# Four open output tiles in block 0, later steps for batches 2 and 3, and a last output tile in two halves

## Chip, cores and metric

The kernel runs on one core of one Trainium2 chip. The metric is the device time of one execution in microseconds. It was run seven times; the profile is of one execution more closely looked at. "PE" is TensorE, "DVE" VectorE, "ACT" ScalarE, "POOL" GpSimd and "SP" the sync engine, whose instructions here are only DMA issues.

## The reference

Linear attention without softmax, a norm over each head, and a two-layer network with a leaky rectifier whose slope differs by column:

```
kv  = einsum('bhsd,bhse->bhde', k, v)          # 8 batches, 8 heads, 576 tokens, head size 64
out = einsum('bhsd,bhde->bhse', q, kv)
rms = sqrt(mean(out*out, axis=-1) + 1e-6)
x   = (out / rms * g_norm)                     # -> 4608 tokens x 512
h   = x @ w_in                                 # 512 x 2048
g   = max(h, 0) + alpha * min(h, 0)
y   = g @ w_out                                # 2048 x 512
```

Inputs and output are float32. The kernel loads with a cast to float16 and multiplies in float16.

## The kernel before

**Tiling.** The 4608 tokens of the output are nine blocks of 512 (`W`, index `w`); a batch has 576, so blocks and batches don't coincide. A block's first product gives 16 groups (`g`) of 128 hidden columns: `m1_group` runs four matmuls into a bank `h_ps`, and `m1_evac` empties it with one ScalarE instruction (`m_sb`) and one VectorE instruction (`gt`). The second product gives four output tiles of 128 tokens (`a`), each a sum of 16 matmuls (`y_mm`) in one bank; `y_out` copies it to SBUF and issues two DMAs on SP, as 64 rows are one run in the output. From block 2 on the loop runs group `g` of block `w` and then four `y_mm` of block `w - 1`. The eight banks of PSUM are three for `h_ps` (`ps_h`), one each in `ps_y` ("y") and `ps_s` ("s"), and three in `ps_o` ("o0" to "o2").

**Attention.** Batches come into two stages in turn by GpSimd DMAs (`load`, two DMAs for each of q, k, v). `regroup` copies q and k from a stage into another order, for batches 0 to 2 on VectorE and later on GpSimd (`regroup_batch`). `step_kv` builds k'v on TensorE, and VectorE masks it into `kv_sb`.

Batches 0 and 1 are transposed on TensorE (`step_t`), and x comes out transposed: `step_ot`, a square on ScalarE or VectorE, `ssq_mm` (a matmul with a mask sums the squares; Ln and Exp on ScalarE give `rstd`) and `norm` on VectorE. From batch 2 on q is transposed by a DMA on SP (`transpose_q`, gives `qtm`), and a tile of 128 tokens passes four steps: `tile_a` (four matmuls `otm_ps`, square on ScalarE into `sqm_sb`), `tile_b` (VectorE reduce into `ss`), `tile_c` (Ln, Exp on ScalarE, then `rg` on GpSimd), `tile_d` (VectorE product `xrow`, then a DMA transpose on SP into `xm`, which the block's first product reads).

**Order.** Nothing is scheduled by the framework: each engine runs its instructions in the order in which the program writes them. The steps of a later block's attention are spread over the loop of block `w` by `phase_steps(w + 1)`: a list of (begin, mid, end), one entry per group, whose parts run before the group, after the group's first product, and after its `y_mm`. Block 2 needs the last 128 tokens of batches 0 and 1 too (`step_tail_ot`, `step_tail_ssq`), so its list starts with these.

**Around the change.** Block 0 runs all its 16 groups first. Then `ahead` runs `y_mm` for three of its four output tiles, interleaved with the attention of batch 1, as filler while TensorE would wait. The fourth tile is done in block 1's loop, one `y_mm` per group. In block 1's loop also stand:

```
            if (w, g) == (1, 1):
                regroup(2, "q"); transpose_q(2)
            if (w, g) == (1, 3):
                nc.gpsimd.tensor_copy(out=gate[:], in_=qtms[2][0:1, 0, 0:1])
                load_batch(3); regroup(2, "k")
            if g == LOAD_G + 3 and w + 2 < B:      # g == 9
                regroup_batch(w + 2)
            if g == NF - 3 and w + 2 < B:          # g == 13
                transpose_q(w + 2)
```

The gate is a tiny GpSimd copy that waits for `qtm` of batch 2, so that the loads behind it on GpSimd start after it.

At the end, block 8's four output tiles run one after the other in the `ps_h` banks.

## Time and profile before

| | us |
|---|---|
| median of 7 runs | 304.66 |
| lowest, highest | 303.16, 305.23 |
| the profiled execution | 305.23 |
| its span in the trace | 303.2 |

| engine | busy, us | share of the span |
|---|---|---|
| PE | 284.8 | 94% |
| DVE | 169.7 | 56% |
| ACT | 152.9 | 50% |
| POOL | 97.8 | 32% |

The span is the traced part of the execution; 2.0 us lie around it. A view that lists instructions gives start and duration in us, the engine, the line, the output and inputs by their names in the program, and in brackets the idle time of the engine just before and what ended it. A wait is put down to the releaser that came last. Matmuls overlap, so one that lasts 0.38 us can be followed by the next after 0.22. The time to landing of a DMA counts from its issue.

### The profile page before, as it was taken

The numbers are of one execution on the slowest core, as the hardware profiler recorded it, in microseconds if no ns is written. First come the engines' busy times: TensorE is split into PE (matmuls) and PEld (weight loads), VectorE is DVE, ScalarE is ACT, GpSimd is POOL, SyncE is SP. The second block draws the span as 40 slices with busy tenths as digits, with TensorE's granted clock in tenths as the row PEclk, the third lists the DMA queues.
The fourth block names the chain that finished last, engine by engine and source line by source line (L and its number), as shares of the span: only waits on it lengthen the run. The fifth ranks groups of instructions, "written<-read, shape, count | busy, mean of one in ns | idle before, by whom it ended". The sixth has DMA issues, their size and how long they took to land.

```text
span 303.2 us, 4249 instructions
## 1 busy us (share of the span) xinstructions
PE 284.8 (94%) x1536; PEld 137.3 (45%) x1536; DVE 169.7 (56%) x261; ACT 152.9 (50%) x297; POOL 97.8 (32%) x109
## 2 busy tenths in 40 slices
PE   5899899883999999999999999999999999999993
PEld 2454444441554455445544544455445444444441
DVE  5469764773486448545963584459546744344200
ACT  1468357462385448435844574458437544434220
POOL 9823410095048414660565054614002300000000
PEclk9999999995799999999999999999999999999998
DMA  7999999699618971995389839935211411122133
GB/s 88 184 206 202 201 204 219 147 138 140 132 27 130 208 173 41 152 224 107 67 120 195 159 75 121 235 90 89 61 35 37 95 35 37 35 46 53 42 69 69
DMA packets 66068, 35.54 MB, mean 117 GB/s; under 512 B 32752, under 2 KB 61440, under 8 KB 66048
## 3 DMA queue, kind: packets, MB, share of 16 engines
q0 software_dynamic: 29664, 18.35, 43.9%
q1 hardware_dynamic: 36384, 16.93, 26.8%
q8 instruction: 12, 0.20, 0.3%
q14 instruction: 8, 0.07, 0.1%
HBM read 36.71 MB, written 9.44 MB: 152 GB/s over the span
## 4 chain that ended last, share of the span: by engine, by line
PE 74%; DMA 13%; issue 8%; POOL 3%; DVE 0%; ACT 0%; POOLq 0%; ACTq 0%
PE y_ps L487 37%; PE h_ps L465 33%; DMA w_in_sb<-in_moe_w_in_dram 5%; DMA w_out_sb<-in_moe_w_out_dram 5%; DMA kst<-in_k_dram 4%; PE otm_ps L387 2%; PE kv_ps L238 2%; POOL w_in_sb L161 1%; POOL qst L96 0%; POOL vst L100 0%; POOL kst L96 0%; POOL qst L100 0%; POOL rg L411 0%; DVE xrow L420 0%; DVE gt L474 0%
## 5 line engine op out<-in xcount | busy, mean ns | idle before, releaser
L474 DVE SCALAR_TENSOR_TENSOR gt<-m_sb,beta_sb,h_ps 128x512 f16<-128x512 f32 x144 | 105.8, 744 | 80.5 <-ACT m_sb L472 80.0
L487 PE MATMUL y_ps<-w_out_sb,gt 128*128 128x512 f16 x528 | 135.6, 380 | 0.0
L472 ACT ACTIVATE m_sb<-h_ps 128x512 f32<-128x512 f32 x144 | 85.5, 597 | 94.3 <-PE h_ps L465 93.7
L465 PE MATMUL h_ps<-xm,w_in_sb 128*128 128x512 f16 x448 | 115.1, 379 | 0.0
L465 PEld LDWEIGHTS <-w_in_sb 128*128 128x128 f16 x584 | 56.2, 99 | 69.1 <-issue 10.9
L487 PEld LDWEIGHTS <-gt 128*128 128x128 f16 x576 | 56.3, 98 | 67.0 <-issue 0.8
L411 POOL TENSOR_TENSOR rg<-ss,g_all 128x512 f32<-128x512 f32 (+1 forms) x30 | 31.2, 1045 | 83.0 <-ACT ss L409 83.0
L465 PE MATMUL h_ps<-xt,w_in_sb 128*128 128x512 f16 (+1 forms) x136 | 33.2, 386 | 6.4 <-DVE gt L474 6.4
L497 ACT COPY y_sb<-y_ps 128x512 f32<-128x512 f32 x33 | 19.2, 582 | 17.4 <-PE y_ps L487 17.1
L399 DVE TENSOR_REDUCE ss<-sqm_sb 128x8 f32<-128x512 f32 (+1 forms) x30 | 20.5, 682 | 9.4 <-ACT sqm_sb L393 9.3
L420 DVE TENSOR_TENSOR xrow<-otm_ps,rg 128x512 f16<-128x512 f32 (+1 forms) x30 | 20.4, 681 | 9.2 <-POOL rg L411 9.2
L393 ACT ACTIVATE sqm_sb<-otm_ps 128x512 f32<-128x512 f32 (+1 forms) x30 | 17.8, 592 | 8.6 <-PE otm_ps L387 8.5
L106 POOL COPY qsb<-qst 128x2560 f16<-128x2560 f16 x5 | 11.6, 2327 | 12.7 <-issue 10.0
L106 POOL COPY ksb<-kst 128x2560 f16<-128x2560 f16 x5 | 11.6, 2321 | 8.8 <-DMA kst<-in_k_dram 8.8
L387 PEld LDWEIGHTS <-qtm 128*128 128x128 f16 x120 | 9.2, 98 | 7.1
L238 PE MATMUL kv_ps<-vst,ksb 128*128 128x128 f16 x160 | 10.4, 219 | 1.7 <-DMA vst<-in_v_dram 1.2
L197 PE MATMUL warm_ps<-warm,mask 128*128 128x512 f16 x26 | 8.7, 474 | 3.3 <-DVE eps_t L140 3.3
L387 PE MATMUL otm_ps<-kv_sb,qtm 128*128 128x128 f16 x120 | 11.6, 219 | 0.0
L406 ACT ACTIVATE ss<-ss,eps_t 128x8 f32<-128x8 f32 (+1 forms) x30 | 9.0, 301 | 4.7 <-DVE ss L399 4.6
L238 PEld LDWEIGHTS <-ksb 128*128 128x128 f16 x160 | 9.3, 98 | 4.5 <-DVE ksb L106 1.4
L242 DVE TENSOR_TENSOR kv_sb<-kv_ps,mask 128x512 f16<-128x512 f32 (+1 forms) x9 | 5.6, 628 | 4.1 <-PE kv_ps L238 4.0
L100 POOL DMA_DIRECT2D vst<-in_v_dram x9 | 6.3, 705 | 3.9 <-DMA w_in_sb<-in_moe_w_in_dram 1.9
(72 smaller groups left out, 124.4 us busy)
## 6 DMA issues: line engine op xcount, KB each, us to landing
out_dram<-y_sb SPq DMA_DIRECT2D x72, 128.0 KB, 2.4
kst<-in_k_dram POOLq DMA_DIRECT2D x7, 320.0 KB, 8.5
qst<-in_q_dram POOLq DMA_DIRECT2D x7, 320.0 KB, 4.9
vst<-in_v_dram POOLq DMA_DIRECT2D x7, 320.0 KB, 10.8
w_in_sb<-in_moe_w_in_dram POOLq DMA_DIRECT2D x4, 512.0 KB, 10.1
w_out_sb<-in_moe_w_out_dram POOLq DMA_DIRECT2D x4, 512.0 KB, 15.2
kst<-in_k_dram POOLq DMA_DIRECT2D x7, 256.0 KB, 9.4
qst<-in_q_dram POOLq DMA_DIRECT2D x7, 256.0 KB, 6.5
```

Source lines behind the costliest of these rows:

```text
L106: (eng or nc.vector).tensor_copy(out=bufs[b % NBUF][nm][:, :, h0:h1, :].rearrange("p t h d -> p h t d"), in_=stages[b % NBUF][nm][:, h0:h1],)
L238: nc.tensor.matmul(out=kv_ps[:, j - j0, :], lhsT=ks(t), rhs=vs(t), start=(t == 0), stop=(t == NT - 1),)
L387: nc.tensor.matmul(out=ot_ps[:, 2 * j : 2 * j + 2, :], lhsT=qtms[b][:, t * NPAIR + j, :], rhs=kvs[b, j], start=True, stop=True,)
L393: nc.scalar.activation(out=sq[0:n], in_=ot_ps[0:n], func=AF.Square)
L399: nc.vector.tensor_reduce(out=ss[0:n], in_=sq[0:n], op=ALU.add, axis=mybir.AxisListType.X,)
L411: nc.gpsimd.tensor_tensor(out=rg[0:n], in0=ss[0:n].unsqueeze(2).to_broadcast([n, H, D]), in1=g_all[0:n].unsqueeze(1).to_broadcast([n, H, D ...
L420: nc.vector.tensor_mul(out=x[0:n], in0=ot_ps[0:n], in1=rg[0:n])
L465: nc.tensor.matmul(out=h_ps[:, cols], lhsT=w_in_blk(c, g), rhs=xt_of(w, c)[:, cols], start=(c == 0), stop=(c == NC - 1 and cols.stop == W),)
L472: nc.scalar.activation(out=m_sb[:], in_=h_ps[:], func=AF.Relu, scale=-1.0)
L474: nc.vector.scalar_tensor_tensor(out=gt[:], in0=m_sb[:], scalar=beta_sb[:, g : g + 1], in1=h_ps[:], op0=ALU.mult, op1=ALU.add,)
L487: nc.tensor.matmul(out=y[:], lhsT=gts[w, g][:, a * P : (a + 1) * P], rhs=w_out_blk(g), start=(g == 0), stop=(g == NF - 1),)
L497: nc.scalar.copy(out=y_sb[:], in_=y[:])
```

## The change

There are three parts.

1. **Start.** The load of the first half of batch 0's q is issued ahead of the construction of `ident` on GpSimd, not after it.
2. **Block 0 to block 2.** `ahead` runs four output tiles, the fourth up to group 11 (`LATER = 12`); its other four `y_mm` stand in groups 0 to 3 of block 1. The tiles' banks are other ones, as are those of batch 1's attention; the three `ps_h` banks get names of their own (`h0` to `h2`) and are dealt out by a counter. Pieces of `ahead` stand before and after `step_kv(1)`, and `step_ot(1, 3)` and the `ssq_mm` stand elsewhere among them. `regroup(2, "q")` and `transpose_q(2)` come before block 0's output copies. In block 1 the load of batch 3 is q and k at group 3 and v at group 9; its regroup stands at group 13 instead of 9, its transpose at 15 instead of 13. In block 2 the steps start two groups later, and `step_kv(3)` stands at group 3 instead of 0.
3. **End.** The last output tile is two sums of 256 columns each, in banks `o0` and `o1`. The first is copied by ScalarE, the second by VectorE, and of each half's two DMAs one is issued on SP and one on ScalarE's queue.

```diff
--- before.py
+++ after.py
@@ -56,7 +56,7 @@
     attn_p = ctx.enter_context(tc.tile_pool(name="attn", bufs=2))
     gt_p = ctx.enter_context(tc.tile_pool(name="gt", bufs=2))
     ysb_p = ctx.enter_context(tc.tile_pool(name="ysb", bufs=4))
-    ps_h = ctx.enter_context(tc.tile_pool(name="psh", bufs=3, space=bass.MemoryType.PSUM))
+    ps_h = ctx.enter_context(tc.tile_pool(name="psh", bufs=1, space=bass.MemoryType.PSUM))
     ps_y = ctx.enter_context(tc.tile_pool(name="psy", bufs=1, space=bass.MemoryType.PSUM))
     ps_s = ctx.enter_context(tc.tile_pool(name="pss", bufs=1, space=bass.MemoryType.PSUM))
     ps_o = ctx.enter_context(tc.tile_pool(name="pso", bufs=1, space=bass.MemoryType.PSUM))
@@ -118,13 +118,15 @@
 
     for nm in "qkv":
         zero_rest(stages[0][nm])
+    HH = H // 2
+    load(0, "q", 0, HH)
 
     ident = const_p.tile([P, P], FP32, name="ident")
     make_identity(nc, ident[:])
-    HH = H // 2
     for h0 in (0, HH):
         for nm in "qkv":
-            load(0, nm, h0, h0 + HH)
+            if (h0, nm) != (0, "q"):
+                load(0, nm, h0, h0 + HH)
 
     mask32 = const_p.tile([P, P], FP32, name="mask32")
     nc.vector.memset(mask32[:], 0.0)
@@ -331,8 +333,6 @@
                 scalar=g2col[:], in1=rstd[:, u, :], op0=ALU.mult, op1=ALU.mult,
             )
 
-    KV_AT = 5
-
 
     TAIL = NB_PE * (S - W)
     JT = min(NPAIR, W // TAIL)
@@ -436,15 +436,16 @@
                 if (b, t) not in done and b * S + t * P < (w + 1) * W]
         done.update(todo)
         steps = []
-        kv_at = 0
+
+        kv_at = {NB_PE: 5, NB_PE + 1: 3}.get(w, 0)
         if w == NB_PE:
             n = NPAIR // JT
             for i in range(n + 1):
                 m = [lambda i=i: step_tail_ot(i)] if i < n else []
                 m += [lambda i=i: step_tail_ssq(i - 1)] if i > 0 else []
                 steps.append(([], [], m))
-            kv_at = KV_AT
-            steps += [([], [], []) for i in range(KV_AT + 2 - len(steps))]
+        n = {NB_PE: 7, NB_PE + 1: 2}.get(w, 0)
+        steps += [([], [], []) for i in range(n - len(steps))]
         for i in range(len(todo) + 2):
             a, b, d = ([todo[i - k]] if 0 <= i - k < len(todo) else [] for k in range(3))
             begin = [lambda x=x: tile_b(*x) for x in b] + [lambda x=x: tile_d(*x) for x in d]
@@ -459,6 +460,7 @@
 
 
     gts = {}
+    H_POOL = [(ps_h, f"h{i}") for i in range(3)]
 
     def m1_mm(h_ps, w, g, cs, cols=slice(0, W)):
         for c in cs:
@@ -477,24 +479,29 @@
         )
         gts[w, g] = gt
 
-    def m1_group(w, g, pool=(ps_h, "h")):
+    n_group = [0]
+
+    def m1_group(w, g, pool=None):
+        if pool is None:
+            pool = H_POOL[n_group[0] % 3]
+            n_group[0] += 1
         h_ps = pool[0].tile([P, W], FP32, name="h_ps", tag=pool[1])
         m1_mm(h_ps, w, g, range(NC))
         m1_evac(h_ps, w, g)
 
 
-    def y_mm(y, w, a, g):
+    def y_mm(y, w, a, g, cols=slice(0, D_MODEL)):
         nc.tensor.matmul(
-            out=y[:], lhsT=gts[w, g][:, a * P : (a + 1) * P], rhs=w_out_blk(g),
+            out=y[:], lhsT=gts[w, g][:, a * P : (a + 1) * P], rhs=w_out_blk(g)[:, cols],
             start=(g == 0), stop=(g == NF - 1),
         )
 
-    def y_out(y, w, a, eng=None):
+    def y_out(y, w, a, eng=None, cols=slice(0, D_MODEL), queues=(nc.sync, nc.sync)):
         y_sb = ysb_p.tile([P, D_MODEL], FP32, name="y_sb")
         if eng is nc.vector:
-            nc.vector.tensor_copy(out=y_sb[:], in_=y[:])
+            nc.vector.tensor_copy(out=y_sb[:, cols], in_=y[:])
         else:
-            nc.scalar.copy(out=y_sb[:], in_=y[:])
+            nc.scalar.copy(out=y_sb[:, cols], in_=y[:])
         for i in range(0, P, REM):
             b, r = divmod(w * W + a * P + i, S)
             t, p = divmod(r, P)
@@ -502,7 +509,9 @@
                 rows = out[b * S : b * S + LONG, :].rearrange("(p t) m -> t p m", t=NT)
             else:
                 rows = out[b * S + LONG : (b + 1) * S, :].rearrange("(p t) m -> t p m", t=TPP)
-            nc.sync.dma_start(out=rows[t], in_=y_sb[i : i + REM, :])
+            queues[i // REM].dma_start(
+                out=rows[t][:, cols], in_=y_sb[i : i + REM, cols],
+            )
 
     g_all = const_p.tile([P, D], FP32, name="g_all")
     diag = const_p.tile([P, D], FP32, name="diag")
@@ -516,15 +525,14 @@
         nc.vector.tensor_copy(out=g_all[:], in_=g_ps[:])
 
 
-    H_POOL = (ps_h, "h")
     O2 = (ps_o, "o2")
     keep_warm(10)
     regroup(0, "q", 0, HH)
     nc.vector.tensor_scalar(
         out=diag[0:D], in0=ident[0:D, 0:D], scalar1=g2col[0:D], scalar2=None, op0=ALU.mult,
     )
-    step_t(0, 0, H_POOL)
-    step_t(0, 1, H_POOL, nc.scalar)
+    step_t(0, 0, H_POOL[0])
+    step_t(0, 1, H_POOL[1], nc.scalar)
     regroup(0, "k", 0, HH)
     keep_warm(8)
     step_kv(0, 0, 2)
@@ -534,9 +542,9 @@
     keep_warm(1)
     regroup(0, "q", HH, H)
     ssq_mm(0, 0)
-    step_t(0, 2, H_POOL)
-    step_t(0, 3, H_POOL)
-    alpha_ps = ps_h.tile([P, NF], FP32, name="alpha_ps", tag="h")
+    step_t(0, 2, H_POOL[2])
+    step_t(0, 3, H_POOL[0])
+    alpha_ps = ps_h.tile([P, NF], FP32, name="alpha_ps", tag="h1")
     nc.tensor.matmul(
         out=alpha_ps[:], lhsT=alpha_row[:], rhs=ident[0:NF, 0:NF], is_transpose=True,
         start=True, stop=True,
@@ -557,7 +565,7 @@
     norm(0, 1)
     half_ot(1, (ps_y, "y"), nc.vector)
     half_ssq(0, O2)
-    first = [ps_h.tile([P, W], FP32, name="h_ps", tag="h") for g in range(3)]
+    first = [ps_h.tile([P, W], FP32, name="h_ps", tag=f"h{g}") for g in range(3)]
     first += [ps_o.tile([P, W], FP32, name="h_ps", tag=f"o{g}") for g in range(2)]
     for g in range(4):
         m1_mm(first[g], 0, g, (0,))
@@ -577,57 +585,66 @@
     others = {5: (ps_s, "s"), 6: (ps_y, "y"), 7: O2, 11: (ps_o, "o0"), 12: (ps_o, "o1"),
               13: (ps_s, "s")}
     for g in range(5, NF):
-        m1_group(0, g, others.get(g, H_POOL))
+        m1_group(0, g, others.get(g))
         if g == 12:
             spread_g()
 
 
 
-    AHEAD = 3
+    LATER = 12
     ys = [
-        ps_y.tile([P, W], FP32, name="ya", tag="y"),
+        ps_h.tile([P, W], FP32, name="ya", tag="h2"),
         ps_o.tile([P, W], FP32, name="yb", tag="o0"),
-        ps_o.tile([P, W], FP32, name="yc", tag="o1"),
+        ps_o.tile([P, W], FP32, name="yc", tag="o2"),
+        ps_y.tile([P, W], FP32, name="yd", tag="y"),
     ]
 
-    def ahead(g0, g1):
+    def ahead(g0, g1, tiles=range(TPW)):
         for g in range(g0, g1):
-            for a in range(AHEAD):
-                y_mm(ys[a], 0, a, g)
+            for a in tiles:
+                if a < TPW - 1 or g < LATER:
+                    y_mm(ys[a], 0, a, g)
 
     S_POOL = (ps_s, "s")
+    O1 = (ps_o, "o1")
     regroup(1, "k")
-    ahead(0, 4)
+    ahead(0, 3)
     regroup(1, "q")
     step_t(1, 0, S_POOL)
-    step_t(1, 1, H_POOL, nc.scalar)
-    step_t(1, 2, H_POOL)
-    step_t(1, 3, H_POOL, nc.scalar)
-    step_kv(1, pool=O2)
-    step_ot(1, 0, S_POOL)
-    step_ot(1, 1, H_POOL)
-    step_ot(1, 2, H_POOL, nc.vector)
-    step_ot(1, 3, H_POOL, nc.vector)
+    step_t(1, 1, O1, nc.scalar)
+    step_t(1, 2, H_POOL[0])
+    step_t(1, 3, H_POOL[1], nc.scalar)
+    ahead(3, 4, range(2))
+    step_kv(1, pool=S_POOL)
+    ahead(3, 4, range(2, TPW))
+    step_ot(1, 0, O1)
+    step_ot(1, 1, H_POOL[0])
+    step_ot(1, 2, H_POOL[1], nc.vector)
     ahead(4, 5)
-    ssq_mm(1, 0)
+    ssq_mm(1, 0, S_POOL)
     ahead(5, 7)
-    ssq_mm(1, 1)
+    ssq_mm(1, 1, S_POOL)
     norm(1, 0)
-    ahead(7, 9)
-    ssq_mm(1, 2)
+    ahead(7, 8)
+    step_ot(1, 3, O1, nc.vector)
     norm(1, 1)
+    ahead(8, 9)
+    ssq_mm(1, 2, S_POOL)
     ahead(9, 11)
-    ssq_mm(1, 3)
+    ssq_mm(1, 3, S_POOL)
     norm(1, 2)
+    ahead(11, NF)
     norm(1, 3)
-    ahead(11, NF)
-    for a in range(AHEAD):
+    regroup(2, "q")
+    transpose_q(2)
+    for a in range(TPW - 1):
         y_out(ys[a], 0, a, nc.vector if a == 1 else None)
 
 
 
 
     LOAD_G = 6
+    n_group[0] = 0
     for w in range(1, NW):
         steps = phase_steps(w + 1)
         for g in range(NF):
@@ -636,42 +653,51 @@
             a, part = divmod(g, TPW)
             parts = range(part * TPW, (part + 1) * TPW)
             if w == 1:
-                a, parts = AHEAD, [g]
+                a, y = TPW - 1, ys[TPW - 1]
+                parts = [LATER + g] if LATER + g < NF else []
             begin, mid, end = steps.pop(0) if steps else ([], [], [])
             for f in begin:
                 f()
             m1_group(w, g)
             for f in mid:
                 f()
-            if parts[0] == 0:
-                pool, tag = ((ps_y, "y"), (ps_s, "s"))[a % 2 if w > 1 else 0]
+            if 0 in parts:
+                pool, tag = ((ps_y, "y"), (ps_s, "s"))[a % 2]
                 y = pool.tile([P, W], FP32, name="y_ps", tag=tag)
             for gg in parts:
                 y_mm(y, w - 1, a, gg)
-            if parts[-1] == NF - 1:
+            if NF - 1 in parts:
                 y_out(y, w - 1, a)
             for f in end:
                 f()
-            if (w, g) == (1, 1):
-                regroup(2, "q")
-                transpose_q(2)
             if (w, g) == (1, 3):
 
 
                 gate = const_p.tile([1, 1], FP16, name="gate")
                 nc.gpsimd.tensor_copy(out=gate[:], in_=qtms[2][0:1, 0, 0:1])
-                load_batch(3)
+                load(3, "q")
+                load(3, "k")
                 regroup(2, "k")
-            if g == LOAD_G + 3 and w + 2 < B:
+            if (w, g) == (1, 9):
+                load(3, "v")
+            if g == (13 if w == 1 else LOAD_G + 3) and w + 2 < B:
                 regroup_batch(w + 2)
-            if g == NF - 3 and w + 2 < B:
+            if g == (15 if w == 1 else NF - 3) and w + 2 < B:
                 transpose_q(w + 2)
-    for a in range(TPW):
-        y = ps_h.tile([P, W], FP32, name="y_ps", tag="h")
+    for a in range(TPW - 1):
+        y = ps_h.tile([P, W], FP32, name="y_ps", tag=H_POOL[(n_group[0] + a) % 3][1])
         for g in range(NF):
             y_mm(y, NW - 1, a, g)
         y_out(y, NW - 1, a)
 
+    for i in range(2):
+        y = ps_o.tile([P, W // 2], FP32, name="y_ps", tag=f"o{i}")
+        cols = slice(i * W // 2, (i + 1) * W // 2)
+        for g in range(NF):
+            y_mm(y, NW - 1, TPW - 1, g, cols)
+        y_out(
+            y, NW - 1, TPW - 1, (nc.scalar, nc.vector)[i], cols, (nc.sync, nc.scalar),
+        )
 
 # ---- launch: one core; inputs and outputs as the reference has them ----
 _INS = ['q', 'k', 'v', 'g_norm', 'moe_w_in', 'moe_w_out', 'moe_alpha']
```

## The prediction

> **What bounds the kernel now.** I read the page's slices first (7.58 us each, tenths busy, granted TensorE clock), then TensorE's waits, then the timeline around the worst of them.
>
> ```profile
> PE   5899899883999999999999999999999999999993
> PEclk9999999995799999999999999999999999999998
> ```
>
> TensorE is full from about 80 us on; what can be won lies in the slices before that, with slice 9 (68 to 76 us) the hole, and in the last slice. Waits of TensorE:
>
> ```profile
> PE h_ps L465 <- DVE gt L474: 6.4, 4, 4.0
> ...
> PE kv_ps L238 <- DMA vst<-in_v_dram: 1.2, 2, 0.8
> PE ot_ps L271 <- DVE kv_sb L242: 0.8, 1, 0.8
> PE qt_ps L214 <- DVE qsb L106: 0.6, 1, 0.6
> ```
>
> The largest is a matmul group that waits for VectorE to free its bank. Why VectorE was late stands in its timeline and GpSimd's (start, duration, idle before):
>
> ```profile
> 66.61 2.37 POOL L106 COPY qsb<-qst 128x2560 f16<-128x2560 f16 x1
> 70.31 2.32 POOL L106 COPY ksb<-kst 128x2560 f16<-128x2560 f16 x1 [1.34 <-DMA kst<-in_k_dram]
> 72.60 1.04 POOL L411 TENSOR_TENSOR rg<-ss,g_all 128x512 f32<-128x512 f32 x1
> ```
> ```profile
> 73.67 0.69 DVE L420 TENSOR_TENSOR xrow<-otm_ps,rg 128x512 f16<-128x512 f32 x1 [4.71 <-POOL rg L411]
> 74.28 1.40 DVE L474 SCALAR_TENSOR_TENSOR gt<-m_sb,beta_sb,h_ps 128x512 f16<-128x512 f32 x2
> ```
>
> Batch 3's k regroup stands on GpSimd ahead of the third rg of batch 2 and waits for k to land at 70.2; rg holds xrow, xrow holds the gt behind it, gt holds the three h banks. TensorE idles from 70.88 to 75.07 and pays again in clock (stretch, then busy time and count per engine; granted clock, DMA share, GB/s last):
>
> ```profile
> 68.00:70.00 2.00, 1.39 (x5) 0.44 (x4) 0.95 (x2) 1.22 (x4) 0.97 (x1) 0.82 1.34 182
> 70.00:72.00 2.00, 1.08 (x3) 0.29 (x2) 0.00 (x0) 0.60 (x1) 1.69 (x1) 0.50 1.33 184
> ...
> 78.00:80.00 2.00, 2.00 (x7) 0.78 (x6) 0.61 (x2) 0.90 (x2) 0.00 (x0) 0.62 1.11 212
> ```
>
> 0.82 and 0.62 put the half clock from 69.3 to 79.5. Sum for block 1 (its first matmul at 49.32, block 2's at 79.29, so 29.97 us): a 512-column matmul starts every 0.216 (ya at 46.08, yc at 49.10: 14 steps); 80 of them 17.26, kv 1.08, tail and tile matmuls 1.08: 19.4. The excess, **10.5**, is gaps of 0.60, 0.54, 1.52, 0.77 and 4.19 (7.6), and half of the 5.8 us in which matmuls ran at half clock (2.9).
>
> **The Trainium skill.** "TensorE: Matmul & The Clock Gate", Part 1: the clock gate judges free-running windows of about 3.4 us and has two states, half and full. The trace agrees: 10.2 us at half is three windows; the one before the drop (65.9 to 69.3) was about 40% issuing, while 35.2 to 38.6, about 55%, cost no clock. Same page, "Architectural detail": VectorE, ScalarE and GpSimd run strictly in order; the rg behind a waiting copy is that. "DMA: Bandwidth & Descriptors", "Issuing engines are not separate DMA queues": a second queue saves only the sequencer's issue time. No ScalarE-issued DMA is in the trace.
>
> **Start: q's first half issued ahead of ident.** q's DMA can issue at 0.74 instead of 1.44; k's at 2.83 as before, since two issues and two small operations only swap. Transfers run without a pause from 3.5 to 54 at about 200 GB/s, and GpSimd waits on landings from 8 us on, so an earlier start can move every later landing, by 0.7 at most. The PE chain takes only part: the filler matmuls end near 9.9 and kv starts at 10.5 when v lands. ident reaches VectorE near 2.7, its cast is at 3.13: hidden. I take **-0.4**, ends -0.6 and +0.1.
>
> **Ahead part.** Today (34.68 is the last filler):
>
> ```profile
> 34.68 0.38 PE L487 MATMUL yc<-w_out_sb,gt 128*128 128x512 f16 x1
> 35.66 1.29 PE L214 MATMUL qt_ps<-ident,qsb 128*128 128x128 f16 x20 [0.60 <-DVE qsb L106]
> 37.76 1.29 PE L238 MATMUL kv_ps<-vst,ksb 128*128 128x128 f16 x20 [0.81 <-DMA vst<-in_v_dram]
> 38.88 0.19 PE L271 MATMUL ot_ps<-qt_sb,kv_sb 128*128 128x64 f16 x1
> 39.83 1.02 PE L271 MATMUL ot_ps<-qt_sb,kv_sb 128*128 128x448 f16 x7 [0.76 <-DVE kv_sb L242]
> ```
>
> ahead(0,3) with four tiles is the same 12 matmuls as ahead(0,4) with three. Two y matmuls (0.43) go into the wait for v and two into the wait for kv_sb: **-0.84**. The moved step_ot(1,3) waits for norm(1,0) to free o1: Ln at 41.73 (0.42 after its matmul), Exp to 43.1, norm to 43.85, against a PE time of 44.34: hidden by 0.5; the four ssq share bank s, each Ln over 0.5 before the next. Twelve y matmuls (2.59) come here from block 1, so block 1 starts at 49.32 + 2.59 - 0.84 = 51.03.
>
> regroup(2,q) then sits at 49.8 on VectorE (q2 landed at 48.3: 33.67 plus 14.6), ahead of yb's copy, which still ends by 51.9, before tail_ot needs o0 at 52.2. transpose_q(2) passes six output DMAs on SP: issued near 50.7 instead of 55.07, while v2 streams until 54.8. Landing took 4.9 to 7.8 in this trace: 56 to 59. The outputs wait 3 to 4 us in four buffers; nobody needs them. GpSimd's gate opens at 57, not 60.08; only q3 and k3 follow (four issues of 0.67), so GpSimd is free by 60, and the first rg is not held until 64.62 as now.
>
> **Block 1.** TensorE's own work is 68 matmuls and the rest: 16.8, so it would end at 67.9. But groups 4 to 15 are 0.86 of TensorE each, against a gt spaced 0.65 plus, on VectorE, k's regroup 0.74, mask 0.69, three reduces of 0.64 and three xrow of 0.60: 12.9 to 12.1, with waits between them. Walking each engine in program order (h end +0.2 to m; m 0.6; gt frees the bank after 0.75; reduce, Ln 0.33, Exp 0.21, rg 1.04, xrow):
> - k2's regroup runs 57.3 to 58.1, so kv(2) waits 0.5; the second h bank costs 0.1.
> - Tile 0: reduce 62.45 (behind gt 7), Exp ends 63.7, rg 64.84, xrow 64.93 (reduce 1 comes first, 64.2); gt 9 65.5 to 66.3. Tile 1: Exp ends 65.5, rg 66.6, xrow 66.8 behind reduce 2 at 66.2; gt 10 67.4 to 68.1.
> - v3's load, two issues (1.4), now stands between the second rg (ends 66.6) and the third: rg 68.1 to 69.15 and xrow 2 at 69.24, where Exp (67.43) alone would give 68.6; gt 11 69.84 to 70.6.
> - Group g takes the bank of g - 3: groups 12, 13, 14 could start at 65.07, 67.19, 69.04 and wait 1.26, 0.99, 1.60 for gt 9, 10, 11. The first matmul of block 2 is at 72.3.
>
> So 10.5 goes and **4.45** comes: what is late next is VectorE, then this rg. Two more. The issuing share in 3.4 us windows falls to 25 to 35% for most phases between 65 and 70.6; with 40% enough before, I expect a drop in over half the cases, 0.6 to 2.3 us each. And block 2 needs the last xm transpose: the earlier two landed at 74.4 and 74.8 just as batch 3's last load did (63.93 + 10.6), so the last lands near v3: issued 67.4, plus the 5.2 that q3 took, 72.6 to 72.9, a wait of 0.6. Together **+1.2**, ends 0 and 4.
>
> q3's and k3's regroup at g 13 and transpose_q(3) at 15 run 69.2 to 73.9 on GpSimd and to about 77 on SP, wanted at 80 and later. kv(3) at g 3 of block 2 (near 79) wants v3: 6 us spare. Two rg of block 2 now follow load_batch(4)'s six issues (4.1) and come about 2.6 late; three h banks of 1.73 cover it.
>
> **Last tile.** Now: copy, two issues in a row on SP, then landing:
>
> ```profile
> 298.48 0.59 ACT L497 COPY y_sb<-y_ps 128x512 f32<-128x512 f32 x1 [2.91 <-PE y_ps L487]
> ```
> ```profile
> 295.59 4.60 SPq L505 DMA_DIRECT2D out_dram<-y_sb  x4
> ```
>
> After: the last matmul ends 0.1 sooner (256 columns 0.272, 512 0.379), VectorE copies 256 columns in about 0.42 (the 128x256 mask product took that) instead of 0.59, and the second issue, 0.57, goes to ScalarE's queue; 32 short matmuls add 0.04. Landing (2.3) with half the bytes I leave. **-0.8**; ends -1.1 and, since ScalarE's issue and one more queue to close are unpriced here, +0.3. The first half's evacuation is covered by the second half's 1.7 us of matmuls.
>
> **Sum:** -10.5 + 4.45 + 1.2 - 0.84 - 0.4 - 0.8 = **-6.9**. The profiled execution took 305.23 (span 303.2), 0.57 above the median of 304.66; 305.23 gives 298.3, the median 297.8. I forecast **297.8**.
>
> **Rivals.**
> - *VectorE's chain is looser* (20%): v3's issues don't hold rg (-0.6), the windows fall well and xm is on time: -10.5 + 3.85 - 2.04 = -8.7, **296.0**, less if waits between VectorE's steps are shorter than walked. For it: rg wants just one GpSimd slot. Against: GpSimd issues took 0.67 each throughout.
> - *The clock stays half for two windows and xm is late* (18%): 2.3 + 1.5 instead of 1.2: -4.3, **300.4**. For it: the windows above.
> - *Slower:* v3's load, now in the middle of the tile chain, delays the last xm transpose, for which all of block 2 waits. If v3 takes the 10.6 that it took behind q and k, xm lands at 78.3, 6.0 late, and the clock adds 1.7: -10.5 + 4.45 + 7.7 - 2.04 = -0.4, **304.3**; from 12 us to landing on it is slower by over 0.9. Against: nothing is queued ahead of it. 4% past that, 4% between.
> - *A part does nothing*, the start above all: 0.4 less, inside the range.
>
> **Numbers.** The forecast's own case has 54%, 296.5 to 299.5; the range, 294.8 to 301.0, reaches into the second and third case. A measurement here can tell 0.3% (0.9 us) from no change: faster 0.92, same 0.04, slower 0.04.
>
> **What would show it.** Right: the wait for kst ahead of ksb no longer holds an rg; block 1 starts near 50.6 and block 2 at 72 to 74 instead of 79.3; waits of h_ps for gt of 3 to 4 us in three or four pieces; v3's issues between two rg; a shorter or no half clock; one DMA at the end on ScalarE's queue, span end about 4.0 after the end of the last matmul, now 4.8. Wrong: block 2 waiting for xm beyond 75, or TensorE waiting in block 1 for qtm or v.

## The result and the profile after

| | before | after |
|---|---|---|
| median, us (runs) | 304.48 (35) | 301.11 (14) |
| lowest, highest | 303.16, 305.60 | 300.33, 304.35 |
| the profiled execution (span) | 305.23 (303.2) | 302.55 (300.6) |

The kernel before was run again beside the one after, so its median is another than the 304.66 of the seven runs. The ratio is 0.9906, 95% interval 0.9886 to 0.9925: faster by 3.4 us by the medians and 2.9 by the ratio, half of the 6.9 forecast or less. The profiled execution is one of the longer ones, so the profile shows 2.7 of the 3.4. In the experiments below one execution of `a_v_late` took 1058 us; its ratio leaves that one out, and without it the median is 303.74.

First the page's slices of the kernel after (7.52 us each): busy tenths of TensorE and its granted clock.

```profile
PE   5899999984999999999999999999999999999994
PEclk9999999999799999999999999999999999999999
```

The hole in slices 8 and 9 (counted from 0) has become shallower and is still there, and so is the loss of clock that follows it. TensorE's waits (sum, times, longest) say that the hole has another owner now:

```profile
PE h_ps L467 <- DVE gt L476: 4.2, 4, 1.6
...
PE h_ps L467 <- DMA xm<-xrow: 2.3, 1, 2.3
PE kv_ps L240 <- DMA vst<-in_v_dram: 0.9, 1, 0.9
PE qt_ps L216 <- DVE qsb L106: 0.5, 1, 0.5
...
PE ot_ps L273 <- DVE kv_sb L244: 0.3, 1, 0.3
```

Before, one wait for gt took 4.0; now the longest for gt is 1.6, and a wait of 2.3 for a DMA transpose has come. The timeline of TensorE over the same stretch puts them in order (start, duration, idle before):

```profile
66.25 1.02 PE L467 MATMUL h_ps<-xt,w_in_sb 128*128 128x512 f16 x4 [1.02 <-DVE gt L476]
68.10 1.02 PE L467 MATMUL h_ps<-xt,w_in_sb 128*128 128x512 f16 x4 [0.83 <-DVE gt L476]
70.73 1.89 PE L467 MATMUL h_ps<-xt,w_in_sb 128*128 128x512 f16 x8 [1.61 <-DVE gt L476]
74.89 1.02 PE L467 MATMUL h_ps<-xm,w_in_sb 128*128 128x512 f16 x4 [2.27 <-DMA xm<-xrow]
```

The first three are groups 12, 13 and 14 of block 1, forecast with waits of 1.26, 0.99 and 1.60. The fourth is block 2's first matmul. The idle time counts from the modelled end of the last matmul, 0.38 after its start, while the next could have followed after 0.22; so each wait costs 0.16 more than its idle time: 1.18, 0.99, 1.77 and 2.43. TensorE could have begun block 2 at 74.89 - 2.43 = 72.46; I had walked to 72.3, and allowed 0.6 for xm. GpSimd's timeline shows v3's load between two rg, where the walk put it:

```profile
65.55 1.04 POOL L411 TENSOR_TENSOR rg<-ss,g_all 128x512 f32<-128x512 f32 x1 [0.73 <-ACT ss L409]
66.82 0.74 POOL L96 DMA_DIRECT2D vst<-in_v_dram  x1 [0.23 <-issue]
67.54 0.70 POOL L100 DMA_DIRECT2D vst<-in_v_dram  x1
68.23 1.07 POOL L411 TENSOR_TENSOR rg<-ss,g_all 128x512 f32<-128x512 f32 x1
```

The second xm transpose was issued at 67.42 and landed at 74.39, the last was issued at 70.05 and landed 4.7 later, at 74.75; v3's load landed between them (67.54 + 7.0 = 74.54). In that stretch the DMA engines were not idle. Queue rows of the DMA view, for 70 to 71 us (packets, MB, share of 16 engines):

```profile
q0 software_dynamic: 292, 0.18, 124.1%
q1 hardware_dynamic: 90, 0.02, 10.8%
```

for 70.6 to 72 us:

```profile
q0 software_dynamic: 304, 0.16, 97.5%
q1 hardware_dynamic: 512, 0.13, 46.3%
```

and for 74 to 75 us:

```profile
q1 hardware_dynamic: 1024, 0.26, 121.9%
```

q0 is the load of v3, q1 the transposes. One xm transpose moves 128 KB, in 512 packets of 256 bytes, so the packets of q1 can be dealt out by counting them in order. The 512 are those of the second xm transpose: it had none before 70.6, 3.2 us after its issue, moved them beside the load in 1.3 us, and landed 2.5 later. The last one moved its 512 from 72.8 to 74.1, and nearly all of the 1024 belong to batch 3's q transpose. With no load in flight (`best3` below) the last one has its first packet 1.2 after its issue, moves in 0.8 and lands 0.5 later. Beside the load most of the delay is thus time in which a transpose moves nothing; for part of it the one before it on the queue was still moving (to 69.2 and to 71.9).

Then the granted clock (stretch, busy time and count per engine; clock, DMA share, GB/s last):

```profile
74.00:76.00 2.00, 1.11 (x5) 0.52 (x6) 0.04 (x1) 0.05 (x1) 0.00 (x0) 0.95 1.24 274
76.00:78.00 2.00, 2.00 (x6) 0.73 (x5) 0.75 (x1) 0.55 (x1) 0.00 (x0) 0.50 0.24 52
78.00:80.00 2.00, 2.00 (x8) 0.72 (x6) 0.01 (x1) 0.60 (x1) 0.00 (x0) 0.70 0.00 0
```

0.1 + 1.0 + 0.6 = 1.7 us of matmul time are lost to the clock, once TensorE is working again. The half clock lasts twice that, 3.4 us, the length of one window in "TensorE: Matmul & The Clock Gate", Part 1, of the Trainium skill.

In block 2 is a wait that the forecast had called covered. TensorE, then VectorE, then GpSimd:

```profile
96.97 1.02 PE L467 MATMUL h_ps<-xm,w_in_sb 128*128 128x512 f16 x4 [0.74 <-DVE gt L476]
```
```profile
95.57 0.69 DVE L420 TENSOR_TENSOR xrow<-otm_ps,rg 128x512 f16<-128x512 f32 x1 [3.17 <-POOL rg L411]
```
```profile
93.73 0.74 POOL L100 DMA_DIRECT2D vst<-in_v_dram  x1
94.42 2.12 POOL L411 TENSOR_TENSOR rg<-ss,g_all 128x512 f32<-128x512 f32 x2
```

The six issues of batch 4's load hold two rg, these hold xrow, xrow holds gt: the chain of block 1 again, 0.74 + 0.16 = 0.9 us of TensorE. At the end the last copy and the second queue:

```profile
295.22 2.31 ACTq L512 DMA_DIRECT2D out_dram<-y_sb  x2
296.58 0.42 DVE L502 COPY y_sb<-y_ps 128x256 f32<-128x256 f32 x1 [13.39 <-PE y_ps L494]
```

From the start of the last copy to the end of the span are 300.6 - 296.58 = 4.02 us; before 303.2 - 298.48 = 4.72.

The sum, profile against profile: block 2 begins 4.40 sooner (79.29 to 74.89); clock and the wait in block 2 take back 1.7 + 0.9; the tail gives 0.7: -2.5, and the spans differ by 2.6.

### The profile page after: what moved, and what is told of

It is laid out like the page before. It is cut to its first block, busy times and chain, and to the rows that moved or that the text cites. A ratio compares the mean times of both kernels' runs of the same rounds, so it can differ in the third digit from the quotient of the medians.

```text
span 300.6 us, 4290 instructions
## 1 busy us (share of the span) xinstructions
PE 283.5 (94%) x1552; PEld 138.3 (46%) x1552; DVE 169.6 (56%) x262; ACT 152.7 (51%) x297; POOL 98.7 (33%) x109
## 4 chain that ended last, share of the span: by engine, by line
PE 82%; POOL 4%; DVE 4%; DMA 3%; issue 2%; ACT 2%; POOLq 0%; DVEq 0%; ACTq 0%
PE h_ps L467 37%; PE y_ps L494 35%; PE kv_ps L240 3%; DMA vst<-in_v_dram 2%; POOL rg L411 2%; PE otm_ps L387 2%; DMA xm<-xrow 2%; DVE gt L476 1%; PE ya L494 1%; PE yb L494 1%; PE yc L494 1%; PE yd L494 1%; POOL vst L96 1%; DVE kv_sb L244 1%; DVE ksb L106 1%
## 5 line engine op out<-in xcount | busy, mean ns | idle before, releaser
L494 PE MATMUL y_ps<-w_out_sb,gt 128*128 128x512 f16 (+1 forms) x528 | 129.7, 374 | 0.0
L494 PEld LDWEIGHTS <-gt 128*128 128x128 f16 x592 | 57.8, 98 | 65.4 <-issue 1.1
L467 PE MATMUL h_ps<-xt,w_in_sb 128*128 128x512 f16 (+1 forms) x136 | 30.3, 366 | 3.5 <-DVE gt L476 3.5
L504 ACT COPY y_sb<-y_ps 128x512 f32<-128x512 f32 (+1 forms) x32 | 18.4, 576 | 16.3 <-PE y_ps L494 16.3
L96 POOL DMA_DIRECT2D qst<-in_q_dram x9 | 7.1, 785 | 3.7 <-DVE gt L476 2.9
```

Source lines behind the costliest of these rows:

```text
L467: nc.tensor.matmul(out=h_ps[:, cols], lhsT=w_in_blk(c, g), rhs=xt_of(w, c)[:, cols], start=(c == 0), stop=(c == NC - 1 and cols.stop == W),)
L494: nc.tensor.matmul(out=y[:], lhsT=gts[w, g][:, a * P : (a + 1) * P], rhs=w_out_blk(g)[:, cols], start=(g == 0), stop=(g == NF - 1),)
L504: nc.scalar.copy(out=y_sb[:, cols], in_=y[:])
```

## The experiments

All ratios are against the kernel before. "After" and "before" name the kernel that was edited.

### What holds block 2: the last xm transpose, or VectorE?

`a_v_late`, from after: v3's load two groups later.

```diff
-            if (w, g) == (1, 9):
+            if (w, g) == (1, 11):
                 load(3, "v")
```

> The changed kernel with v of batch 3 loaded at group 11 of block 1, behind the third rg, instead of group 9. Theory A (the last xm transpose lands only when v3 has landed, because both share the DMA engines): the third rg starts near 67.5 instead of 68.2, the last xrow near 68.7 instead of 69.3, its transpose is alone and lands within 2.4 to 4 us, so block 2's first matmul comes at 72 to 73 instead of 74.9; 2.0 to 2.8 us less, and up to 1.7 more if the half clock after it goes too. Theory B (the transposes are slow by themselves or behind each other on SP): the last one still takes 4.7, block 2 starts at 74 or later, under 1 us is won. Theory C (VectorE's three waits alone bring the half clock): the 3.4 us at half clock stay wherever block 2 starts.

303.81 us, ratio 0.9968 (0.9947 to 0.9990), so none of the gain of theory A. rg was freed, the sum of waits for gt fell from 4.2 to 3.4, and all of it and more came back as a longer wait for xm:

```profile
75.83 1.44 PE L467 MATMUL h_ps<-xm,w_in_sb 128*128 128x512 f16 x3 [4.22 <-DMA xm<-xrow]
```

The last xm transpose was issued 1 us sooner than in after (69.0) and landed 0.9 later (75.7), just ahead of v3 (75.9). The one before it had landed at 70.4, so it was not held by that one (theory B). The landing of the load decides, not the issue of the transpose.

`a_v_with_qk`, from after: v3's load back to group 3, behind q and k.

```diff
-                load(3, "q")
-                load(3, "k")
+                load_batch(3)
...
-            if (w, g) == (1, 9):
-                load(3, "v")
```

> The changed kernel with v of batch 3 loaded at group 3 of block 1 together with q and k, as the kernel before does; the late regroup stays. Theory A: v3 lands before 70, the first xm transpose (65.6) lands late with it, the last is issued near 69.5 and lands near 72; block 2 at 72 to 73, the same gain as with v at group 11: 2 to 4 us. Theory B: no change, within 0.6 us. If GpSimd's six issues in a row hold the first rg (they would end near 61.7, rg is wanted at 63.8), VectorE waits there and the gain is smaller by that.

302.21, ratio 0.9908 (0.9884 to 0.9931): the same as after by the ratios, whose intervals overlap. Waits for gt fell to 2.6, as the order on GpSimd said, but v3, forecast before 70, still landed at 74.2 (62.24 + 12.0), the last xm at 75.8, and xm was waited for 2.0. This profile lost 0.8 in the start and two windows of clock as well, so it says little on its own.

`a_v_block2`, from after: v3's load behind the tile chain and behind batch 3's regroup; batch 3's kv then later in block 2, in bank `y`, which is free there.

```diff
-        kv_at = {NB_PE: 5, NB_PE + 1: 3}.get(w, 0)
+        kv_at = {NB_PE: 5, NB_PE + 1: 6}.get(w, 0)
...
-        n = {NB_PE: 7, NB_PE + 1: 2}.get(w, 0)
+        n = {NB_PE: 7, NB_PE + 1: 5}.get(w, 0)
...
-            if (w, g) == (1, 9):
+            if (w, g) == (1, 14):
                 load(3, "v")
```

> The changed kernel with v of batch 3 loaded at group 14 of block 1, behind batch 3's regroup on GpSimd, and the steps of block 2 three groups later still (step_kv(3) at group 6 in bank y). No load is in flight when the last xm transpose is issued. Theory A (a DMA transpose advances only when the load queue is empty: with v at 9, 11 and 3 the last one landed 0.2 us after, 0.3 before and 1.6 after v3's end): it lands in about 2.4 us, near 71.5, and block 2 starts at 72.0, 2.9 us earlier. Batch 4's load issues follow v3's while GpSimd is idle, so no rg stands behind them and the 0.74 us wait in block 2 goes too: 3 to 4 us less in all. Theory B (the transpose is slow behind its two predecessors): it still takes 4.5 and block 2 starts at 74. Against both: v3 or kv_sb of batch 3 late, then TensorE waits for v in block 2.

298.93, ratio 0.9809 (0.9784 to 0.9834). Block 2's first matmul, with no wait:

```profile
72.03 1.02 PE L467 MATMUL h_ps<-xm,w_in_sb 128*128 128x512 f16 x4
```

The last xm transpose was issued at 69.49 and landed in 2.4 us with no load in flight, as theory A said, and the clock stayed full. The reason that theory A gives is too strong: after's second xm transpose did move its packets beside a load. TensorE reaches block 2 where the walk of the prediction had it (72.3, and this start was no earlier). New is a wait of 1.45 near 100 us: the last rg of block 2 now stands behind batch 4's regroup (q's copy at 93.03, k's at 95.29, rg at 97.57).

### What the half clock costs

`a_filler`, from after: matmuls of constants into the free bank `y` before groups 12, 13 and 14 of block 1 and before block 2; nothing of the computation changes.

```diff
+    WARM_AT = {(1, 12): 4, (1, 13): 4, (1, 14): 6, (2, 0): 8}
...
+            if (w, g) in WARM_AT:
+                wp = ps_y.tile([P, W], FP32, name="warm2", tag="y")
+                for i in range(WARM_AT[w, g]):
+                    nc.tensor.matmul(out=wp[:], lhsT=mask16[:], rhs=warm16[:], start=True, stop=True)
             m1_group(w, g)
```

> The changed kernel with 4, 4, 6 and 8 matmuls of constants into a free bank ahead of groups 12, 13 and 14 of block 1 and group 0 of block 2, where TensorE waits; they need 0.86, 0.86, 1.3 and 1.7 us of waits of 1.0, 0.8, 1.6 and 2.3. Theory A (the clock gate saw too few matmuls in one window): the clock stays 1.00, block 2's first groups take 1.73 each, 1.7 us less in executions that fell to half clock, so the median falls by 0.5 to 1.5 and the spread (300.3 to 304.4) shrinks. Theory B (the half clock has another cause): it stays, no change or a few tenths slower.

301.07, ratio 0.9890 (0.9867 to 0.9914), 300.47 to 302.19, with a mean granted clock of 0.997 to 1.000 in every execution. The profiled one took 301.01, 1.5 less than after's, about the 1.7 of its half clock; but the median is that of after. Among after's own 15 executions, the profiled one counted, 13 have a mean clock of 0.977 to 0.994, the fastest two (300.33; 0.985 and 0.994) among them, and the two at 0.999 took 300.96 and 301.26. So the half clock is in after's profile, and the median's shortfall is not explained by it. What makes after's runs spread over 4.0 us is open: only one of them has a trace. In `a_v_late`, with its longer hole, time and clock go together: 300.78 to 302.21 in the five executions at 0.999, 302.86 to 305.23 in those below. A longer hole also lowers the clock, so how much of that is the clock itself is not shown.

### The start

`a_ident_first`, from after, and `b_q_first`, from before: the start undone, and the start alone.

```diff
-    HH = H // 2
-    load(0, "q", 0, HH)
     ident = const_p.tile([P, P], FP32, name="ident")
     make_identity(nc, ident[:])
+    HH = H // 2
     for h0 in (0, HH):
         for nm in "qkv":
-            if (h0, nm) != (0, "q"):
-                load(0, nm, h0, h0 + HH)
+            load(0, nm, h0, h0 + HH)
```

> The changed kernel with the start undone: ident is built ahead of the first load on GpSimd. Theory A (k's and v's issues come 0.36 later behind the early q, and they, not q, are waited for): first kv matmul at 10.5 instead of 10.9, and about 0.4 us less up to block 0's first matmul; less than 0.4 in the end, since the waits for batch 1 give some back. Theory B (the first landings just differ from run to run): kv stays near 10.9, no change.

> The kernel before with the start alone: q's first half is loaded ahead of ident. Theory A (every kernel with this order had its first landing at 5.4 to 5.5 instead of 4.8 to 4.9, and k's and v's issues 0.36 later): first ya near 32.8 instead of 32.3, 0.2 to 0.6 slower. Theory B (those runs differ for another reason): equal within 0.2.

`a_ident_first`: 300.14, ratio 0.9880 (0.9847 to 0.9914); `b_q_first`: 305.06, ratio 1.0021 (1.0007 to 1.0035). Both say that this part costs, by the ratios, some 0.6 to 0.8 us; the interval of the first overlaps that of after, and that of the second only just leaves out no change. GpSimd's timeline of after:

```profile
1.25 0.81 POOL L96 DMA_DIRECT2D qst<-in_q_dram  x1 [0.80 <-POOLq L714]
...
3.19 0.61 POOL L96 DMA_DIRECT2D kst<-in_k_dram  x1
```

and of `a_ident_first`:

```profile
1.45 0.80 POOL L96 DMA_DIRECT2D qst<-in_q_dram  x1
...
2.83 0.63 POOL L96 DMA_DIRECT2D kst<-in_k_dram  x1
```

q's issue moves by 0.2, not 0.7: in all eight kernels that begin with q, its DMA starts at 1.25 after a wait of 0.8 for GpSimd's sequencer, while ident, where it comes first, starts at 0.74. So ident ran within that wait; now it stands ahead of k, which is issued 0.36 later. And the first landing takes 4.2 from its issue where it took 3.4. From 3.5 to 4 us the load queue had this in before, then in after:

```profile
q0 software_dynamic: 138, 0.09, 122.5%
```
```profile
q0 software_dynamic: 48, 0.03, 41.0%
```

The first ya matmul stands at 32.1 on average in the six kernels that begin with ident and have a profile here (31.70 to 32.39), at 32.8 in the eight that begin with q (32.39 to 33.43). Up to 4.0 us the queue had moved 176 packets in before and 83 in after, and q's first DMA alone has 256 (160 KB, 640 bytes each). So it is most likely q's own DMA that moves more slowly here, though it was issued sooner, and not the later k that is missing. Why is open, and what the later k costs is not separated from it.

`a_ident_first` also waits 2.0 for xm and 4.2 for gt, like after, and keeps the full clock. Its windows:

```profile
72.00:74.00 2.00, 0.37 (x2) 0.22 (x3) 0.97 (x2) 0.31 (x1) 0.86 (x1) 1.00 1.38 213
74.00:76.00 2.00, 2.00 (x12) 0.88 (x10) 0.68 (x1) 0.60 (x1) 0.00 (x0) 1.00 0.77 161
76.00:78.00 2.00, 2.00 (x11) 0.94 (x10) 0.81 (x2) 0.60 (x1) 0.00 (x0) 1.00 0.00 0
```

Almost the same hole (1.61 and 1.95 of waits, for 1.61 and 2.27), 0.9 to 1.3 us sooner, cost no clock. Where the clock may change can be read from the traces: in after it changes at 75.78, at 79.20 and as the work ends, whole multiples of 3.413 us apart. In the three stretches of that length before after's drop (65.5 to 75.8) TensorE was busy for 55%, 53% and 34%. Counted back from the change at its end, the same three in `a_ident_first` (65.6 to 75.8) had 51%, 55% and 65%: the wait for xm, which lies in one stretch in after, is split between two. Over all fourteen profiles, up to the last matmul, the half clock followed every full-clock stretch in which TensorE was busy for under 46%, and none above that (the nearest are 45.8% in `a_v_with_qk` and 46.05% in `b_order`).

### Block 2's load and the tail

`a_load4_g9`, from after: batch 4's load in block 2 at group 9, out of the way of the two rg.

```diff
-            if g == LOAD_G and 3 < w + 2 < B:
+            if g == (9 if w == 2 else LOAD_G) and 3 < w + 2 < B:
```

> The changed kernel with batch 4's load in block 2 at group 9 instead of 6, behind the last two rg of that block. Theory A: the 0.74 us that TensorE waits for gt near 96 is the rg that stands behind six load issues; it goes, 0.9 us less and no new wait. Theory B: later loading makes batch 4's regroup late, its transposed q or k comes late, and a wait of the same size appears in block 3: no change or slower.

305.22, ratio 1.0019 (0.9997 to 1.0042): all of the change's gain gone. The wait for gt went, as theory A said, and batch 4's kv, in block 3, had to wait for the load that I had moved, as theory B said:

```profile
109.95 1.94 PE L240 MATMUL kv_ps<-vst,ksb 128*128 128x128 f16 x20 [2.45 <-DMA vst<-in_v_dram]
```

In this profile the clock was then half from 110.4 to 113.8 as well, which is another 1.7 us.

`a_tail_whole`, from after: the last tile as one, as before.

```diff
-    for a in range(TPW - 1):
+    for a in range(TPW):
...
-    for i in range(2):
-        ... (the two halves)
```

> The changed kernel with the last output tile whole again, copied by ScalarE and stored by two DMAs on SP. If the halves are worth what the profiles say (last matmul to span end 4.8 before, 4.1 after): 0.7 to 0.8 us slower than the changed kernel. If the second queue costs something outside the span: less than 0.4 slower.

302.65, ratio 0.9921 (0.9890 to 0.9951). From the start of the last copy to the end: 301.1 - 296.37 = 4.73, the 4.72 of before. The two halves are worth 0.7 by the profiles, 0.0015 of 304.5, 0.5, by the ratios, whose intervals overlap, and 1.5 by the medians; the size is thus known from the profiles alone.

### How much of the change was needed

`b_regroup_g13`, from before: only the regroup and the transpose of batch 3 moved.

```diff
-            if g == LOAD_G + 3 and w + 2 < B:
+            if g == (13 if w == 1 else LOAD_G + 3) and w + 2 < B:
...
-            if g == NF - 3 and w + 2 < B:
+            if g == (15 if w == 1 else NF - 3) and w + 2 < B:
```

> The kernel before with one edit: in block 1 batch 3's regroup at group 13 instead of 9 and its transpose at 15 instead of 13. Theory A (that order on GpSimd was the hole): the wait of 4.19 goes, waits of 1.5 and 0.8 near 66 to 69 stay, the last xm lands with v3 near 75, block 2 starts near 75.5 instead of 79.3: 3 to 4.5 us less, as much as the whole change won. Theory B (the other parts of the change carry half of it): 1.5 to 2 us less.

302.74, ratio 0.9932 (0.9909 to 0.9955): 1.7 to 2.1 of the 2.9 to 3.4 us that the whole change brings, with no other part of it. That is the time of theory B, with block 2's start near that of theory A: block 2 begins at 75.05, after at 74.89, held by the same transpose:

```profile
75.05 1.02 PE L465 MATMUL h_ps<-xm,w_in_sb 128*128 128x512 f16 x4 [2.65 <-DMA xm<-xrow]
```

`b_order`, from before: block 0 untouched, only the order for batches 3 and 4, with v3 behind the tile chain.

```diff
-                load_batch(3)
+                load(3, "q")
+                load(3, "k")
                 regroup(2, "k")
+            if (w, g) == (1, 14):
+                load(3, "v")
-            if g == LOAD_G + 3 and w + 2 < B:
+            if g == {1: 13, 2: 11}.get(w, LOAD_G + 3) and w + 2 < B:
                 regroup_batch(w + 2)
-            if g == NF - 3 and w + 2 < B:
+            if g == {1: 15, 2: 14}.get(w, NF - 3) and w + 2 < B:
                 transpose_q(w + 2)
```

Block 2's steps start five groups later, and `step_kv(3)` stands at its group 6 in bank `y`.

> The kernel before with the order of batch 3 and 4 alone: q and k of batch 3 at group 3, v at group 14, its regroup at 13 and transpose at 15, block 2's steps five groups later with step_kv(3) at group 6 in bank y, batch 4's regroup at 11 and transpose at 14. Three open tiles, the late q regroup of batch 2 and the whole last tile stay. Theory A (in block 1 VectorE's chain and the last xm set the end, so the four tiles' 1.3 us in block 0 are lost there): block 2 starts at 71 to 72, and it is 0.5 to 1.0 slower than the kernel with all of it, by the last tile: 297.4 to 297.9. Theory B (the four tiles' gain is kept): block 2 starts at 72.7 or later, 1.8 to 2.2 slower: 298.7 to 299.1.

302.13, ratio 0.9926 (0.9899 to 0.9954). Block 2 begins at 71.94, 7.3 sooner than before, as theory A said, and then comes a wait that neither theory had: TensorE waits for q of batch 3. SP's timeline, and TensorE's:

```profile
72.58 1.12 SPq L507 DMA_DIRECT2D out_dram<-y_sb  x2
73.79 8.18 SPq L377 DMA_TRANSPOSE qtm<-qsb  x1
```
```profile
90.73 0.40 PE L387 MATMUL otm_ps<-kv_sb,qtm 128*128 128x128 f16 x4 [3.25 <-DMA qtm<-qsb]
```

On SP the transpose stands behind the output of block 0's fourth tile, which this kernel finishes at group 15. GpSimd issues eight loads beside it (72.71 to 78.2), and it took 16.9 us to land.

`b_order2`, from `b_order`: that transpose one group earlier, ahead of the output.

```diff
-            if g == {1: 15, 2: 14}.get(w, NF - 3) and w + 2 < B:
+            if g == {1: 14, 2: 14}.get(w, NF - 3) and w + 2 < B:
                 transpose_q(w + 2)
```

> The kernel before with only the order of batches 3 and 4 changed (q and k at group 3, v at 14, regroup at 13, later steps in block 2), and batch 3's q transpose at group 14 of block 1 instead of 15, so that on the sync queue it stands ahead of the output of block 0's fourth tile. In the run with 15 it was issued behind that output at 73.8 us and took 16.9 us to land, and TensorE waited 3.2 us for it in block 2. Theory A (the queue's order is all that is wrong with that version; the four open tiles bring it nothing else that can be measured): the wait of 3.2 us goes, block 2's first matmul stays near 71.9, median 298.4 to 299.3 (302.13 less 2.8 to 3.7). Theory B (the transpose lands late because of the loads that run beside it, wherever it is issued; without four open tiles it can't come early enough): the wait stays over 1.5 us and the median at 300.5 or more.

297.65, ratio 0.9777 (0.9753 to 0.9801), 4.5 less than `b_order` for one number in the program. SP's timeline:

```profile
69.96 3.10 SPq L377 DMA_TRANSPOSE qtm<-qsb  x1
73.16 7.17 SPq L507 DMA_DIRECT2D out_dram<-y_sb  x4
```

It landed in 7.5 us, and TensorE doesn't wait at all between 76 and 110. Theory A expected 298.4 to 299.3, so it is better than even the theory that the queue's order is all that was wrong. With block 0, start and tail as before, it gains twice what the change gains.

`best3`: after, with `a_v_block2`'s edits, ident first, and batch 4's regroup at group 11 of block 2 (its transpose at 14), behind the last rg.

> The kernel with v of batch 3 at group 14 and later steps in block 2, with two edits more: ident ahead of the first load again, and batch 4's regroup at group 11 of block 2 instead of 9 (its transpose at 14), behind the last rg of that block. Theory A: the start gives 0.6 (first ya at 32.3 instead of 32.9), and the wait of 1.4 us near 98 to 102, where an rg stood behind batch 4's regroup, goes: 296.9, 2 us less than that kernel. Theory B: the start only differs from run to run: 297.5; or the later regroup makes kv of batch 4 wait in block 3: 298 or more.

296.37 (295.88 to 297.23), ratio 0.9744 (0.9723 to 0.9765), the fastest. Block 2 begins at 70.64. Slices of its page (7.34 us each):

```profile
PE   5899999987999999999999999999999999999994
PEclk9999999999999999999999999999999999999999
```

Against `b_order2` it has the four open tiles and the tail: 1.6 us of span, 0.85 of it at the start of block 2 (71.49 and 70.64; 0.26 of these already at the first ya) and 0.7 in the tail. The four tiles, with what goes with them, are thus worth about 0.6 by these two profiles; no run has them alone. Taking twelve matmuls out of block 1 leaves TensorE less to do while VectorE works: waits for gt sum to 1.6 in `b_order2` and to 2.6 in `best3`.

## Why the prediction was wrong

The direction was right, and so was the walk through block 1. The gain was half of the forecast, because the prediction let the last xm transpose land 5.2 us after v3's issue and took 0.6 for it, took nothing for block 2's late rg, took too little for the clock, and had the start the wrong way round. In its own terms:

- **The excess of block 1 and VectorE's waits (-10.5 + 4.45): right.** Waits of 1.18, 0.99 and 1.77 for 1.26, 0.99 and 1.60; rg at 63.78, 65.55 and 68.23; TensorE ready at 72.46 for 72.3. `a_v_block2` begins block 2 at 72.03.
- **xm (+0.6): the step that failed most.** I took v3's landing as 5.2, from q3, and the transpose as landing with it. It does land with it, but v3 took 7.0, so the transpose landed at 74.75 and not by 72.9, and the wait was 2.43. The rival on the other side had the right mechanism, a load in the middle of the tile chain that delays the last xm; `a_v_late` shows how little more is needed: two groups, and two thirds of the gain are gone. "DMA: Bandwidth & Descriptors", "Queues, rings and completion order", in the Trainium skill, says that a DMA engine takes turns between the queues that it has work for, a packet from each. Here the packets of the two did mix, 304 to 512 from 70.6 to 72; but the delay lies mostly before a transpose's first packet and after its last, and why is not shown.
- **Clock (+0.6): undersized for the execution profiled**, 1.7, in one window. In the median it costs nothing that `a_filler` could bring back.
- **Block 2's two late rg (0, "three h banks of 1.73 cover it"): wrong**, 0.9. I compared the 2.6 by which the rg are late with the depth of the banks, and left out that two xrow and a gt then queue on VectorE, as in block 1.
- **Start (-0.4): wrong in sign**, +0.6 to +0.8. I took the issue at 0.74 from the place of ident's first instruction, but with q first the DMA issue waits for GpSimd's sequencer to 1.25; and "two issues and two small operations only swap" missed that ident had been inside that wait.
- **Ahead (-0.84): right in kind, and larger.** From the first ya to block 1 are 51.00 - 32.67 = 18.33; before, with the twelve moved matmuls, 17.02 + 2.59 = 19.61: -1.28. But by `b_order2` and `best3` about half of it is lost again to VectorE in block 1.
- **Tail (-0.8): right**, -0.70.
- **Two slips of the working, without weight:** 49.32 + 2.59 - 0.84 is 51.07, not 51.03; and the second xm transpose of the kernel before landed at 74.95, not 74.8.

For the profiled execution the forecast was 298.3, and it took 302.55, 4.25 more. Against the forecast the terms are +1.8 for xm, +1.1 for the clock, +0.9 for block 2, +0.8 for the start (32.30 to 32.67 at the first ya, for -0.4), +0.1 for block 1 (72.46 - 51.00 = 21.46, for 29.97 - 2.59 - 10.5 + 4.45 = 21.33), +0.1 for the tail and -0.4 for ahead: 4.4, near enough to 4.25. The median, 301.11, is 3.3 above the forecast of 297.8 and 0.1 above the range; which of these terms are smaller in the shorter runs is not shown. Nearest is the rival with half clock and a late xm (300.4), whose two terms were 2.3 and 1.5 where the profile has 1.7 and 2.4.

## What to carry to other kernels

A DMA transpose that the next stage waits for was priced here by the loads in flight beside it, not by its own length: ask when the load queue is empty, and put loads behind the last transpose, and a transpose ahead of outputs on its queue. Follow a moved load to what it now stands ahead of on the issuing engine: 0.7 us per issue in front of a short operation can hold three engines. And before a large reordering, try its smallest part alone: two numbers, moved by four groups and by two, gave over half of this one.

## What the runs showed of the hardware

- Landing of one 128x512 xm transpose: 2.4 us with no load in flight (`best3` and `a_v_block2`, the last before block 2), 4.7 in after and 6.6 in `a_v_late` beside v3's load. A transpose of q: 4.9 in before with no load beside it, 7.5 with loads issued behind it (`b_order2`), and 16.9 beside eight load issues (`b_order`).
- The half clock depends on how a hole falls into stretches of 3.4 us, not on its size alone: after lost 1.7 us of clock with a stretch that was 34% busy; `a_ident_first`, with nearly the same hole 0.9 to 1.3 us sooner and no stretch under 51%, none. Over the fourteen profiles the limit lies at 46% busy.
- A first DMA issued at 1.25 landed at 5.4 to 5.5 (eight kernels), issued at 1.44 at 4.8 to 5.0 (six): the earlier issue came later.
